# Threshold attention with a feed-forward block on one core: earlier front ends, one product with v a round later, and q and k turned in other rounds

## The chip, the cores and the metric

The kernel runs on one core of a Trainium2 chip. The metric is the device time of one execution in microseconds (us). Before the change three runs gave 907.24, 909.61 and 909.83 us, median 909.61. The profiled execution spans 909.1 us.

## The reference

Eight batches of eight heads, 576 positions, 64 numbers per head, all float32. Then a feed-forward block over the 4,608 tokens of 512 numbers.

```python
scores = (1 / sqrt(64)) * q @ k.T                     # per batch and head, 576 x 576
thresh = max(scores, axis=-1) - tau
scores = where(scores >= thresh, scores, -1e9)
attn   = exp(scores - max(scores))
attn   = attn / (sum(attn) + 1e-9)
x      = attn @ v                                     # -> tokens x 512
h      = x @ w_in                                     # 512 -> 1024
solu   = h * softmax(h)
ln     = (solu - mean(solu)) / sqrt(var(solu) + 1e-6) * g_ln
out    = ln @ w_out                                   # 1024 -> 512
```

The weights w_in, w_out and g_ln arrive as 64-bit numbers and are converted in the kernel.

## The kernel before

All five engines follow one order, written out by hand in a loop of rounds (`while True`, L748). A slot is 128 query rows of a pair of heads; there are 18 per batch (`PER`), 144 in all (`NS`). In each batch four pairs of heads have two slots for the first 256 rows (kind 0), two for the next 256 (kind 1), and two last slots (kind 2) hold the remaining 64 rows of all four pairs. The 64 last rows of every head, named `ends` in the code, are called front ends below, after the words that describe the change.

Round `rnd` does this, in program order. PE turns some blocks of q and k into the spare columns of the score banks (`turn`, L269) and computes the scores of slot `rnd` (`scores`, L396). DVE finds each row's negated threshold (`maxes`, L413), ACT makes the ramp (`ramp`, L424) and the exponentials with their sums (`exps`, L433). Between the ramps of the two heads the turned blocks are copied out (`keeps`): q by L302 and L306, k by L327, the front ends by L343 and L347. These copies are divided between ACT and DVE, and stay wholly on ACT up to round 16 (`eased`). POOL normalises the slot of the round before (L443), DVE transposes it in 32 x 32 blocks (L455), and after the second slot of a unit SP issues four transfers that put the blocks into the order of the product with v (`wT<-T`, L466, 288 KB each).

The score banks are single (`s0`, `s1`): the next round's turns and scores wait until the ramps of this round have read them. The two other pairs of banks (`p0`, `p1`) are handed out by `take` and given back by `pairs_free`.

A unit is the two slots of one pair. Its product with v (`attend`, L491) is due `LAG_PV` = 3 rounds after its second slot; for the first two units one round more (`pv_due`, L687). Products with v come on PE after the round's scores and its feed-forward quarter, and may share a round with a quarter of the first kind only. When the four units of a batch and kind are done, two feed-forward tiles of 128 tokens become ready. A tile has four quarters, one per round: two of h = x w_in (L545) and two of the product with w_out (L647). Between them lie an exponential (L567), statistics on DVE (L588), a chain of small operations on POOL, the normalisation on ACT (L609) and on DVE (L614), a swap of halves by transfers (`V<-u`, L625) and a transposition (L635). So most rounds have a quarter, and some have none.

When a batch's q and k are turned is fixed by `preps` (L693): each pair has an earliest round `at` and four pieces, k in 3 and 1 blocks, one of front ends and 4 of q. A round takes pieces in order while its seven spare blocks (`SPARE`) last. A round in which a tile is in its second half takes none as long as the pair's first slot is more than four rounds off.

At the start `load_qk(0, 0)` loads q on SP's queue and k on ACT's, in halves of two heads; after the first half come the front ends of all eight heads (L135), and after these the second halves. Then tau is loaded (L724), and the first three weight pieces on ACT's queue. `whole_pair(0)` turns all of pair 0 in one go, into a pair of banks of its own; its copies need the scale that DVE derives from tau (`scl`, L174). Pairs 1 to 3 of batch 0 are turned whole in rounds 0, 2 and 4. During rounds 0 to 15 DVE also converts one weight piece per round (L221 to L247), each loaded three rounds ahead.

Of the kernel before, what the change touches and what calls it, by code (L numbers as in the profile page):

```python
# [16 lines left out]
P = 128  # L17
# [3 lines left out]
def kernel(  # L21
# [27 lines left out]
    nc = tc.nc  # L49
    B, H, S, D = q.shape  # L50
    DM, DFF = w_in.shape
    SM = 512
    ST = S - SM
    NP = H // 2
# [5 lines left out]
    ROWS = (slice(0, 64), slice(64, P))  # L60
# [15 lines left out]
    tau_t = const.tile([P, 1], F32, name="tau_t")  # L76
# [14 lines left out]
    ends = {}  # L91
# [27 lines left out]
    def load_one(b, hf, nm, queue=None):  # L119
        d = halves.setdefault((b, hf), {})  # L120
        hs = slice(4 * hf, 4 * hf + 4)
        src, rows = {"q": (q, ROWS[0]), "k": (k, ROWS[1])}[nm]
        d[nm] = loads.tile([P, 4, 4, D], F32, tag=nm, name=nm)

        parts = [slice(0, 2), slice(2, 4)] if b == 0 and hf == 0 else [slice(0, 4)]
        for x, part in enumerate(parts):
            queue = nc.scalar if nm == "k" and x + 1 < len(parts) else nc.sync
            queue.dma_start(
                out=d[nm][:, part].rearrange("p h t d -> p h (t d)"),
                in_=src[b, hs, 0:SM, :][part].rearrange("h (p t) d -> p h (t d)", t=4),  # L130
            )
            if hf == 0 and x == 0:
                if b not in ends:
                    ends[b] = loads.tile([P, H, D], F32, tag="ends", name="ends")
                queue.dma_start(  # L135
                    out=ends[b][rows], in_=src[b, :, SM:S, :].rearrange("h p d -> p h d")
                )

    def load_qk(b, hf):
        load_one(b, hf, "q")  # L140
        load_one(b, hf, "k")
# [52 lines left out]
    def piece(x):  # L194
        if x < 2 * NP:
            c, hf = divmod(x, 2)
            cols = slice(512 * hf, 512 * hf + 512)
            return w_in[P * c : P * c + P, cols], w1[:, c, cols], W_UNIT
        c = x - 2 * NP
        return w_out[P * c : P * c + P], w2[:, 2 * c], gs[:, c : c + 1]  # L200
# [4 lines left out]
    def weight_load(x):  # L205
        raw = work.tile(
            [P, 512], I64 if wide else F32, tag=("xh2", "xh3", "uT")[x % 3], bufs=1, name="raw"
        )
        queue = nc.scalar if x < 3 else nc.sync
        queue.dma_start(out=raw, in_=piece(x)[0])  # L210
        raws[x] = dict(raw=raw)
# [79 lines left out]
    def q_item(i, ts=slice(0, 4)):  # L291
        src, h0 = source(i)
        qT = pair(i)["qT"].rearrange("p (t r k) -> p r t k", t=4, r=2)
        n = ts.stop - ts.start

        def make(spare, x):
            for t in range(n):
                turn(spare, x + t, lambda r, y: src["q"][ROWS[r], h0 + y, ts.start + t])

        def keep(spare, x, r):  # L300
            if r == 0 or spare.get("eased"):
                nc.scalar.activation(  # L302
                    out=qT[:, r, ts], in_=seen(spare, r, x, n), func=AF.Copy, scale=scl
                )
            else:
                nc.vector.tensor_scalar(  # L306
                    out=qT[:, 1, ts], in0=seen(spare, 1, x, n), scalar1=scl, scalar2=None,
                    op0=ALU.mult,
                )

        return n, make, keep
# [5 lines left out]
    def k_item(i, ts=slice(0, 4)):  # L317
        src, h0 = source(i)
        to = k_parts(i)
        n = ts.stop - ts.start  # L320

        def make(spare, x):
            for t in range(n):
                turn(spare, x + t, lambda r, y: src["k"][ROWS[r], h0 + y, ts.start + t])

        def keep(spare, x, r):
            (nc.vector.tensor_copy if r and not spare.get("eased") else nc.scalar.copy)(  # L327
                out=to[:, 4 * r + ts.start : 4 * r + ts.stop],
                in_=seen(spare, r, x, n).rearrange("p t (k c) -> p t c k", c=2),
            )  # L330

        return n, make, keep

    def e_item(i):
        src, h0 = source(i)
        last = k_parts(i)[:, NK - 1]

        def make(spare, x):
            turn(spare, x, lambda r, y: ends[i // NP][ROWS[r], 2 * (i % NP) + y])

        def keep(spare, x, r):
            if r == 0:
                nc.scalar.activation(  # L343
                    out=pair(i)["qe"], in_=seen(spare, 0, x, 1)[:, 0], func=AF.Copy, scale=scl
                )
            else:
                (nc.scalar.copy if spare.get("eased") else nc.vector.tensor_copy)(  # L347
                    out=last, in_=seen(spare, 1, x, 1)[:, 0].rearrange("p (k c) -> p c k", c=2)
                )

        return 1, make, keep
# [329 lines left out]
    PER = NS // B  # L681
    LAG_PV = 3

    pv_due = []
    for s, (b, kind, hp, r) in enumerate(slots):
        if r == 1:
            pv_due.append((s + LAG_PV + (s < 4), (b, kind, hp)))  # L687

    def first_slot(i):
        return PER * (i // NP) + 2 * (i % NP)  # L690
# [2 lines left out]
    preps = []  # L693
    for i in range(NP, NPAIR):
        b, hp = divmod(i, NP)
        at = 13 + 2 * hp if i < 2 * NP - 1 else PER * (b - 1) + (6 + 3 * hp if hp < 3 else PER - 1)
        preps += [
            (at, 3, lambda i=i: k_item(i, slice(0, 3)), i),
            (at, 1, lambda i=i: k_item(i, slice(3, 4)), i),
            (at, 1, lambda i=i: e_item(i), i),  # L700
            (at, 4, lambda i=i: q_item(i), i),
        ]

    load_at = {}
    for b in range(1, B):
        r = PER * (b - 1)

        for at, job, hf, what in (
            (-1 if b > 1 else 11, load_one, 0, "q"),
            (1 if b > 1 else 9, load_one, 0, "k"),  # L710
            (7 if b > 1 else 13, load_one, 1, "k"),
            (9 if b > 1 else 15, load_one, 1, "q"),
            (11 if b > 1 else 17, load_v, 0, (0,)),
            (13 if b > 1 else 19, load_v, 0, (1, 2)),
            (PER + 3, load_v, 1, (0,)),
            (PER + 5, load_v, 1, (1, 2)),
        ):
            load_at.setdefault(r + at, []).append(
                lambda b=b, job=job, hf=hf, what=what: job(b, hf, what)
            )  # L720

    with tc.manual_schedule():
        load_qk(0, 0)
        nc.scalar.dma_start(out=tau_t, in_=tau.partition_broadcast(P))  # L724
        weight_load(0)
        constants()
        for x in range(1, 3):
            weight_load(x)
        load_qk(0, 1)
        nc.sync.dma_start(out=g_rows, in_=g_ln.rearrange("(c p) -> c p", p=P))  # L730
        whole_pair(0)
# [16 lines left out]
        while True:  # L748
# [70 lines left out]
            elif step == ("h", 1):  # L819
# [8 lines left out]
                at = rnd + 4 if more or not ready else rnd + 6  # L828
# [16 lines left out]
            if attending is not None:  # L845
                attend(attending)
                attended(attending)
                b, kind, hp = attending
# [56 lines left out]
```

## Time and profile before

| stretch (us) | PE busy | DVE busy | ACT busy | granted PE clock | DMA share |
|---|---|---|---|---|---|
| 10 to 20 | 5.66 | 7.14 | 6.63 | 0.89 | 0.81 |
| 20 to 30 | 6.24 | 9.82 | 8.48 | 0.67 | 0.74 |
| 50 to 60 | 5.75 | 9.93 | 7.56 | 0.84 | 0.90 |
| 100 to 110 | 10.00 | 8.37 | 7.09 | 1.00 | 0.76 |
| 120 to 130 | 8.73 | 8.02 | 8.74 | 1.00 | 0.68 |
| 150 to 160 | 10.00 | 6.76 | 7.25 | 1.00 | 1.01 |
| 190 to 200 | 8.60 | 2.91 | 2.84 | 0.83 | 1.03 |

Each row is ten microseconds; a busy time near ten names the engine that is the bound there. The granted clock is the mean share of full speed at which PE ran. The DMA share is the mean busy share of the 16 transfer engines. Lines of a timeline read: start, length, engine, source line, operation, tile written and read, shape, count, and in brackets the idle time before it with what ended that. One matmul instruction of float32 leaves two records, so counts of records are twice those of instructions.

### The profile page before, as it was taken

Reading aid. Unit: us, or ns where it says so; the run is one execution under the profiler, and the core shown is the slowest. Engines: PE = TensorE matmul, PEld = TensorE weight load, DVE = VectorE, ACT = ScalarE, POOL = GpSimd, SP = SyncE. Lnnn points to the kernel's source line nnn. Section 1 sums busy time; section 2 is a strip of 40 time slices with the busy share of each in tenths; the row PEclk is TensorE's granted clock in tenths of the full one; section 3 lists DMA queues with packets and bytes.
Section 4 is the critical chain, followed back from the end, with each engine's and each line's share of the span. In section 5 each row is a group of like instructions: output and inputs, shape, how many; then the busy total and the mean of one; then the engine's idle time right before and its main releaser. Section 6 shows DMA issues by size and latency. Waiting matters only on the chain. (4 is left out here: it accounts for less than half of the span.)

```text
span 909.1 us, 39662 instructions
## 1 busy us (share of the span) xinstructions
PE 852.8 (94%) x17089; PEld 653.6 (72%) x17089; DVE 679.3 (75%) x1307; ACT 591.6 (65%) x1239; POOL 453.8 (50%) x870
## 2 busy tenths in 40 slices
PE   4667799989999999999999999999999999999997
PEld 3444567878668787877788776888878778777555
DVE  4999877868767877787767777777777777777351
ACT  4867776757666766677757776777767777666121
POOL 1645555545645555555545455555555555555120
PEclk8679899999999999999999999999999999999999
DMA  7999979776867777777767777776877756766322
GB/s 222 251 224 255 212 186 208 183 173 155 196 144 181 172 166 184 180 174 166 185 161 173 175 161 170 183 172 158 191 175 176 177 136 152 169 143 139 81 48 48
DMA packets 95470, 154.61 MB, mean 170 GB/s; under 512 B 27192, under 2 KB 69184, under 8 KB 95296
## 3 DMA queue, kind: packets, MB, share of 16 engines
q1 hardware_dynamic: 93920, 150.12, 70.7%
q8 instruction: 134, 2.20, 1.1%
q10 hardware_dynamic: 1376, 1.97, 0.7%
q14 instruction: 40, 0.33, 0.1%
HBM read 46.14 MB, written 9.44 MB: 61 GB/s over the span
## 5 line engine op out<-in xcount | busy, mean ns | idle before, releaser
L413 DVE CUSTOM_DVE_ANT_0 w<-s_ps,tau_t 128x576 f32<-128x576 f32 x288 | 206.7, 755 | 159.2 <-PE s_ps L396 125.8
L424 ACT ACTIVATE w<-s_ps,nth 128x576 f32<-128x576 f32 x288 | 207.7, 744 | 122.0 <-DVE nth L413 99.3
L647 PE MATMUL o_ps<-w,uT 64*64 64x256 f32 x4608 | 270.5, 376 | 2.9 <-issue 1.8
L647 PEld LDWEIGHTS o_ps<-w,uT 64*64 64x64 f32 x4608 | 231.4, 133 | 48.8 <-issue 11.4
L545 PE MATMUL h_ps<-w,xh 64*64 64x512 f32 x1856 | 222.3, 593 | 3.4 <-issue 3.4
L443 POOL TENSOR_SCALAR w<-w,sm 128x576 f32<-128x576 f32 x288 | 218.2, 770 | 14.3
L433 ACT ACTIVATE w<-w,ntau 128x576 f32<-128x576 f32 x288 | 220.2, 772 | 0.0
L455 DVE STREAM_TRANSPOSE T<-w 128x576 f32<-128x576 f32 x288 | 205.7, 750 | 4.4 <-POOL w L443 4.0
L491 PEld LDWEIGHTS pv<-wT,v 64*64 64x64 f32 x5760 | 174.3, 138 | 38.5 <-issue 23.5
L396 PE MATMUL s_ps<-kT,qT 64*64 64x64 f32 (+1 forms) x2048 | 175.8, 421 | 15.0 <-ACT w L424 13.1
L491 PE MATMUL pv<-wT,v 64*64 64x128 f32 (+1 forms) x5760 | 176.1, 267 | 10.2 <-DMA wT<-T 6.2
L545 PEld LDWEIGHTS h_ps<-w,xh 64*64 64x64 f32 x1856 | 120.8, 134 | 87.2 <-issue 56.2
L440 POOL TENSOR_SCALAR sm<-sm 128x2 f32<-128x2 f32 x144 | 36.2, 252 | 277.6 <-ACT w L433 274.9
L441 POOL TENSOR_TENSOR sm<-sm,mone 128x2 f32<-128x2 f32 x144 | 107.9, 749 | 12.0
L396 PEld LDWEIGHTS s_ps<-kT,qT 64*64 64x64 f32 x2048 | 67.8, 138 | 23.7 <-ACT w L424 19.4
L609 ACT ACTIVATE V<-u,nb,rs 128x1024 f32<-128x1024 f32 x36 | 44.7, 1241 | 52.6 <-POOL nb L599 52.6
L513 ACT COPY xh<-pv 128x256 f32<-128x256 f32 x64 | 23.8, 373 | 73.8 <-PE pv L491 73.8
L433 ACT ACTIVATION_READ_ACCUMULATOR w<-w,ntau 128x1 f32 x288 | 56.8, 197 | 0.0
L558 DVE TENSOR_REDUCE hm<-h_ps 128x1 f32<-128x1024 f32 x36 | 43.0, 1194 | 12.7 <-PE h_ps L545 6.8
L573 DVE TENSOR_TENSOR u<-h_ps,u 128x1024 f32<-128x1024 f32 x36 | 42.8, 1190 | 10.3 <-ACT u L567 10.3
L635 DVE STREAM_TRANSPOSE uT<-V 128x1024 f32<-128x1024 f32 x36 | 43.8, 1217 | 8.9 <-DMA V<-u 8.8
L567 ACT ACTIVATE u<-h_ps,hm 128x1024 f32<-128x1024 f32 x36 | 40.3, 1119 | 13.8 <-DVE hm L558 8.0
(74 smaller groups left out, 620.0 us busy)
## 6 DMA issues: line engine op xcount, KB each, us to landing
wT<-T SPq DMA_DIRECT2D x288, 288.0 KB, 5.7
V<-u SPq DMA_DIRECT2D x144, 64.0 KB, 3.6
out_dram<-ob SPq DMA_DIRECT2D x72, 128.0 KB, 3.1
v<-in_v_dram SPq DMA_DIRECT2D x16, 512.0 KB, 6.2
v<-in_v_dram SPq DMA_DIRECT2D x32, 256.0 KB, 6.0
q<-in_q_dram SPq DMA_DIRECT2D x15, 512.0 KB, 6.8
k<-in_k_dram SPq DMA_DIRECT2D x15, 512.0 KB, 6.4
raw<-in_moe_w_out_dram SPq DMA_DIRECT2D x8, 512.0 KB, 6.8
```

What stands on the lines that cost most here:

```text
L396: nc.tensor.matmul(out=ps[h][ROWS[y], ks], lhsT=lhsT, rhs=d["kT"][ROWS[h], ks], start=True, stop=True,)
L413: nc.vector.tensor_tensor_reduce(out=w, in0=ps[:, 0:S], in1=tau_t.to_broadcast([P, S]), scale=1.0, scalar=BIG, op0=ALU.add, op1=ALU.min, a ...
L424: nc.scalar.activation(out=d["w"][x], in_=d["ps"][x][:, 0:S], func=AF.Prelu, bias=d["nth"][x], scale=-1.0, alpha=1.0e30,)
L433: nc.scalar.activation(out=w, in_=w, func=AF.Exp, bias=ntau, scale=1.0, accum_out=sm[:, x : x + 1])
L441: nc.gpsimd.tensor_tensor(out=sm, in0=sm, in1=mone, op=ALU.pow)
L443: nc.gpsimd.tensor_scalar(out=w, in0=w, scalar1=sm[:, x : x + 1], scalar2=1.0, op0=ALU.mult, op1=ALU.mult)
L455: nc.vector.transpose(out=T[:, :, r, h, :], in_=w)
L491: nc.tensor.matmul(out=to, lhsT=d["v"][ROWS[u], h0 + h, m ^ 4 * u if m < 8 else m], rhs=rhs, start=m == 0, stop=m == NK - 1,)
L545: mm = nc.tensor.matmul(out=h[ROWS[y], f], lhsT=x[ROWS[r], c, ROWS[y]], rhs=w1_parts[ROWS[r], c, part ^ r], start=part == 0 and c == 0, st ...
L609: nc.scalar.activation(out=V, in_=u, func=AF.Identity, bias=nb, scale=rs)
L635: nc.vector.transpose(out=uT, in_=d["V"].rearrange("p y (m x) -> p m y x", x=32))
L647: nc.tensor.matmul(out=d["o"][ROWS[z], 512 * r : 512 * r + 256], lhsT=d["uT"][ROWS[r], m].rearrange("p y x -> p (y x)"), rhs=w2[ROWS[r], m ...
```

## The change

Three things are moved; nothing is computed differently.

First, the start. Tau's load goes ahead of q and k on ACT's queue. The front ends are loaded in two parts for batch 0: those of heads 0 and 1 where all eight were, the other six on SP's queue after the first weight loads and before `load_qk(0, 1)`. It is meant to bring what the first pair needs sooner.

Second, `(s < 4)` becomes `(s < 6)`: the third unit's product with v is due four rounds after its second slot and not three, in round 9 and not 8, which gives its transfers more time.

Third, new earliest rounds for the turns of batches 1 and 2; from batch 3 on they are as before. By the written order, in batch 1 pair 2 moves from rounds 18 and 19 to 20 and 21, and pair 3 from 19 and 20 to 21 and 22. In batch 2 pair 1 moves from rounds 28 and 29 to 30 and 31, pair 2 from 30 and 31 to 34 and 35, pair 3 from 35 and 38 to 39 and 40. It is meant to keep turns out of rounds that have no feed-forward quarter.

```diff
-                queue.dma_start(
-                    out=ends[b][rows], in_=src[b, :, SM:S, :].rearrange("h p d -> p h d")
-                )
+                load_ends(b, nm, slice(0, 2) if len(parts) > 1 else slice(0, H), queue)
+
+    def load_ends(b, nm, of, queue):
+        src, rows = {"q": (q, ROWS[0]), "k": (k, ROWS[1])}[nm]
+        queue.dma_start(
+            out=ends[b][rows, of], in_=src[b, of, SM:S, :].rearrange("h p d -> p h d")
+        )
...
-            pv_due.append((s + LAG_PV + (s < 4), (b, kind, hp)))
+            pv_due.append((s + LAG_PV + (s < 6), (b, kind, hp)))
...
-        at = 13 + 2 * hp if i < 2 * NP - 1 else PER * (b - 1) + (6 + 3 * hp if hp < 3 else PER - 1)
+        if b == 1:
+            at = (13, 15, 20, 20)[hp]
+        else:
+            at = PER * (b - 1) + ((6, 12, 16, 21) if b == 2 else (6, 9, 12, 17))[hp]
...
     with tc.manual_schedule():
+        nc.scalar.dma_start(out=tau_t, in_=tau.partition_broadcast(P))
         load_qk(0, 0)
-        nc.scalar.dma_start(out=tau_t, in_=tau.partition_broadcast(P))
         weight_load(0)
         constants()
         for x in range(1, 3):
             weight_load(x)
+        for nm in ("q", "k"):
+            load_ends(0, nm, slice(2, H), nc.sync)
         load_qk(0, 1)
```

## Prediction

> **What bounds the kernel now.** I read the page first, busy time and the 40 slices, then busy time by stretch, then the engines' timelines over the first 260 us.
>
> ```profile
> PE 852.8 (94%) x17089; PEld 653.6 (72%) x17089; DVE 679.3 (75%) x1307; ACT 591.6 (65%) x1239; POOL 453.8 (50%) x870
> ...
> PE   4667799989999999999999999999999999999997
> ...
> DVE  4999877868767877787767777777777777777351
> ```
> ```profile
> 0.00:110.00 110.00, 73.16 (x1263) 48.46 (x1267) 93.69 (x194) 73.44 (x162) 53.37 (x83) 0.81 0.91 231
> ```
> ```profile
> 110.00:250.00 140.00, 132.06 (x2846) 103.87 (x2842) 103.97 (x205) 95.33 (x205) 73.22 (x140) 0.99 0.80 186
> ```
> ```profile
> 250.00:800.00 550.00, 544.34 (x11373) 431.62 (x11369) 424.10 (x824) 382.36 (x800) 292.64 (x573) 1.00 0.74 170
> ```
> The columns of a stretch are its length, then busy time of PE, weight loads, DVE, ACT and POOL, granted clock, DMA share and GB/s. So there are three stages. To about 105 us DVE is the bound (93.69 of 110 us, and most of the rest is the start): each round holds 5.35 us of DVE work, of which nearly half is the conversion of a weight piece. From 110 to 250 us PE is busy all but 7.9 us. From 250 us on PE is full (5.7 us of 550 idle, gaps put down to "issue"). A microsecond taken from the DVE path before 105 us moves all that follows; one taken from PE work after it counts too; idle PE time before 105 us is worth nothing by itself.
>
> Where does DVE wait in the first stage? At the start, and at two places for the scores:
>
> ```profile
> 7.45 0.15 DVE L174 TENSOR_SCALAR scl<-tau_t 128x1 f32<-128x1 f32 x1 [7.45 <-DMA tau_t<-in_tau_dram]
> ...
> 45.45 0.76 DVE L413 CUSTOM_DVE_ANT_0 w<-s_ps,tau_t 128x576 f32<-128x576 f32 x1 [0.67 <-PE s_ps L396]
> 63.24 0.76 DVE L413 CUSTOM_DVE_ANT_0 w<-s_ps,tau_t 128x576 f32<-128x576 f32 x1 [1.81 <-PE s_ps L396]
> ```
> PE's timeline says what held the scores in each case:
>
> ```profile
> 5.13 1.10 PE L269 MATMUL tp<-ident,k 64*64 64x64 f32 x32
> 8.33 0.49 PE L269 MATMUL tp<-ident,ends 64*64 64x64 f32 x8 [2.09 <-DMA ends<-in_q_dram]
> 10.00 2.20 PE L396 MATMUL s_ps<-kT,qT 64*64 64x64 f32 x16 [1.19 <-DVE kT L347]
> ...
> 56.97 0.43 PE L491 MATMUL pv<-wT,v 64*64 64x128 f32 x4 [2.72 <-DMA wT<-T]
> 58.58 3.74 PE L491 MATMUL pv<-wT,v 64*64 64x128 f32 x66 [1.18 <-DMA wT<-T]
> ```
> The first two heads' q and k are turned by 6.2 us, then PE stands until the front ends of q have landed at 8.3. At 57 us the product of unit (0,0,2) with v heads PE's queue and waits 3.9 us for its transposed weights; the next scores are queued behind it, and DVE loses 1.81 us.
>
> **What the skill says.** "DMA: Bandwidth & Descriptors", under "Why small descriptors are slow (HBM only)", says that pieces of 256 B carry a fixed overhead, 27% of the bus time. A front end is 512 rows of 256 B, and the trace agrees in kind: q's 128 KB were issued at 1.23 us and needed until 8.3, while 256 KB of k issued at 0.72 had landed 4.0 us later. The same page, "Issuing engines are not separate DMA queues": transfers of SP and ACT interleave on the same engines, so an earlier place only helps what is small or early. "TensorE: Matmul & The Clock Gate", "HAM oscillation": PE idle for some 3.4 us falls to a slower clock. Here the products with v took 3.74 us at 191.83 after an idle 1.53, and 2.23 at 163.19 with none, so a shorter gap than the page's is enough here.
>
> **Part 1, start.** Tau goes first on ACT's queue; only two heads of each front end (32 KB instead of 128) go ahead of the second half of q and k; six heads follow. Gain: the front ends can no longer be the last to land, since q lands at 4.1 and k at 4.7 (issue plus 3.4 and 4.0), k perhaps 0.3 later behind tau's issue (0.63 us). k's turns end at about 6.2 instead of the front ends starting at 8.33, so up to 8.33 - 6.2 = 2.1 us. Tau, landed at 7.4 before, must not take its place: first in its queue and 0.5 KB, it should be there by 4. I take 2.0 us, bounds 1.0 and 2.3. It is on the path, because scores, the first maxima (DVE, 12.23) and all rounds of the DVE-bound stage follow in a chain. Costs: two more issues on SP (0.7 us each), off the path while q and k of the second half land only at 10.0 and 10.6. In the built program transfers share eight completion lanes in turn, so the six heads wait for tau and for q, which are early, and k of the second four heads now waits for a lane that is free only when q of heads 2 and 3 has landed, about 10 us instead of 5.2. It is used at 23 us, and landed at 17.6 before: hidden. The six heads are needed by the turns of pair 1, before at 13.65, now at 11.6; the scores behind those turns wait for a ramp until 15.5 - 2 = 13.5, so a landing up to 13 is hidden. What could give part of it back is DMA, whose share is about 1.0 between 30 and 50 us; but transposed weights issued at 29.6 landed 6.6 us later at 36.2, 3.3 us before their use at 39.5, and these issues move along with the rounds.
>
> **Part 2, third unit's product from round 8 to round 9.** It then follows the scores of round 9, whose ramp ends at 58.3 (both before the shift of part 1). Those scores end at 59.5 instead of 63.3, so DVE's 1.81 us go. The product starts near 59.5, when the last quarter of its weights has landed (issue about 51.3 plus 7.3 is 58.6), so its own wait goes too. Give-back: one round later the next unit's product comes directly behind in PE's order, in round 10. Before, it started at 67.35 with 1.7 us to spare for the scores behind it (they ended at 72.1, DVE came to them at 73.9); its weights, issued until 62.9, land no earlier through this part. So of the 1.81 up to 0.5 may return as a wait. I take 1.5, bounds 0.8 and 1.9. The output copy on ACT moves with it, and the first feed-forward tile needs only the fourth unit: no cost.
>
> **Part 3, the turns.** No work is added or removed. Pairs 2 and 3 of batch 1 leave rounds 18 to 20 for 20 to 22; of batch 2, pair 1 leaves rounds 28 and 29 for 30 and 31, pair 2 goes from 30 and 31 to 34 and 35, pair 3 from 35 and 38 to 39 and 40. Rounds 19, 28, 29 and 38 have no feed-forward quarter, so PE comes to their end early and waits for ramps, which stand behind the copies of the turned blocks on ACT:
>
> ```profile
> 127.54 0.33 PE L269 MATMUL s_ps<-ident,k 64*64 64x64 f32 x4 [0.89 <-ACT kT L327]
> ...
> 178.80 0.33 PE L269 MATMUL s_ps<-ident,q 64*64 64x64 f32 x4 [0.93 <-ACT qe L343]
> ...
> 191.00 0.44 PE L491 MATMUL pv<-wT,v 64*64 64x128 f32 x4 [1.53 <-DMA wT<-T]
> 191.83 3.74 PE L491 MATMUL pv<-wT,v 64*64 64x128 f32 x66 [0.40 <-DMA wT<-T]
> ```
> Rounds 18 to 20: turns of 0.58 and 0.82 us leave PE, copies of 0.79 leave ACT. But round 19's ramps also stand behind the normalisation on ACT, which waits for POOL until 124.56 and moves with DVE by only 0.7 to 0.9. I get the ramp's end at 126.65 for 128.1: 1.5 us sooner. Rounds 21 and 22, where PE has no idle time, take 0.82 + 0.72 = 1.54 us more. Net 0.
>
> Rounds 28 to 30: the scores of round 30 come 2.1 us sooner. Then a wait takes the place: the product of round 30 needs weights whose transfer is issued behind DVE's transposition (178.96) and the swap of the normalised tile (179.06), which move by 0.8 only. PE would wait about 2.8 us instead of 1.53, and 0.8 us is left, against 0.58 + 0.47 added to rounds 34 to 40 (0.58 of pair 2 and the net 0.47 of pair 3, the rest being exchanged) with 0.4 recovered in round 38. Net +0.2, bounds -1.0 and +1.5. The sum for part 3 is taken as 0.
>
> **Sum.** 909.6 - 2.0 - 1.5 + 0 = 906.1 us.
>
> **Rivals.** (a) The turns pay: PE's idle time in rounds 19, 20, 28, 29 and 38 (0.89 + 0.31 + 0.93 + 0.30 + 0.17 + 0.40 + 0.87 = 3.9 us) largely goes, without the new wait. With 2.5 of it: 903.6. Against it speaks the wait at 191. (b) The start's gain is lost to DMA, or unit 4's wait returns all of part 2: 909.6 - 1.0 - 0.8 + 0.5 = 908.3, within 0.3%. For it: the DMA share. Against: weight loads issued at 67 landed in 3.6 us, so no backlog builds up before then. (c) Slower: the moved turns (2.9 us of PE work in all) land in full rounds, PE stands still longer at 191 and runs cold for a further stretch (1.5 us, as 3.74 against 2.23), 0.5 of part 2 returns, and only 1.8 is gained before: 909.6 + 2.9 + 1.5 + 0.5 - 1.8 = 912.7.
>
> **Chances.** Forecast 0.57, (a) 0.12, (b) 0.21, (c) 0.10. Runs of the kernel before lie within 907.2 to 909.8, so any of these blurs by about 1 us. Faster by over 0.3% means under 906.9: most of the forecast and (a), 0.66. Slower means over 912.3: 0.10. The rest, 0.24, is no change. The range takes in (a) and (b) and stops short of (c): 903.4 to 910.0.
>
> **What would show it.** Right: front-end turns at about 6.2 us with no long wait; first maximum near 10.2; no wait of DVE for scores in round 9; DVE's 110 us of work done some 3.5 us sooner; idle PE at about 127 and 179 smaller, at about 190 larger; rounds 250 us on unchanged in length. Wrong: tau or k as the new last lander, a wait of the fourth unit of over 1 us in which DVE stands still, or a gap at the third batch's pair in 30 to 40 that grows.

## The result and the profile after

The changed kernel took 902.5 us (median of four runs, 901.9 to 904.4) against 909.7 for the kernel before on the same chip (907.2 to 910.2): ratio 0.993, interval 0.9906 to 0.9953. That is 7.2 us by the medians, where 3.5 were forecast, and 0.9 us below the low end of the range. Three later measurements of the same kernel gave 0.9969, 1.0005 and 0.9942. So there are two questions: what the change does, and why one measurement does not tell it.

First the pair of traces on record. The page after, busy time and then the 40 slices of PE and DVE:

```profile
PE 847.8 (94%) x17089; PEld 658.4 (73%) x17089; DVE 680.1 (76%) x1307; ACT 591.9 (66%) x1239; POOL 452.7 (50%) x870
...
PE   5667889999899999999999999999999999999997
...
DVE  5999878878677777777777877777877877787351
```
Busy time by stretch after, with the columns of the prediction (length, PE, weight loads, DVE, ACT, POOL, granted clock, DMA share, GB/s):

```profile
0.00:110.00 110.00, 76.03 (x1349) 51.73 (x1353) 95.64 (x195) 75.44 (x166) 53.48 (x84) 0.80 0.91 238
110.00:250.00 140.00, 131.49 (x2883) 105.93 (x2879) 107.08 (x210) 97.91 (x209) 74.87 (x143) 1.00 0.81 191
250.00:800.00 550.00, 545.58 (x11433) 438.76 (x11429) 426.96 (x829) 383.12 (x801) 294.84 (x579) 1.00 0.73 170
```
More DVE work fits into the first 110 us (95.64 for 93.69) and the next 140 (107.08 for 103.97). From 250 us on PE is as full as before. So the time came for the most part from the first 250 us, as the argument wanted. Where in them, the timeline of PE after tells, at the places shown of before:

```profile
4.91 1.13 PE L273 MATMUL tp<-ident,q 64*64 64x64 f32 x32 [4.91 <-DMA q<-in_q_dram]
5.79 1.10 PE L273 MATMUL tp<-ident,k 64*64 64x64 f32 x32
6.64 0.46 PE L273 MATMUL tp<-ident,ends 64*64 64x64 f32 x8
...
64.94 0.43 PE L495 MATMUL pv<-wT,v 64*64 64x128 f32 x4 [1.66 <-DMA wT<-T]
66.23 2.07 PE L495 MATMUL pv<-wT,v 64*64 64x128 f32 x66 [0.86 <-DMA wT<-T]
...
122.78 0.33 PE L273 MATMUL s_ps<-ident,k 64*64 64x64 f32 x4 [0.94 <-ACT w L428]
...
133.08 0.27 PE L273 MATMUL s_ps<-ident,k 64*64 64x64 f32 x1 [1.50 <-issue]
133.19 1.19 PE L400 MATMUL s_ps<-kT,qT 64*64 64x64 f32 x13
134.11 3.70 PE L549 MATMUL h_ps<-w,xh 64*64 64x512 f32 x32
...
173.91 0.33 PE L400 MATMUL s_ps<-kT,qT 64*64 64x64 f32 x4 [0.94 <-ACT w L428]
...
183.99 0.44 PE L495 MATMUL pv<-wT,v 64*64 64x128 f32 x4 [0.77 <-DMA wT<-T]
185.48 2.07 PE L495 MATMUL pv<-wT,v 64*64 64x128 f32 x66 [1.06 <-DMA wT<-T]
```
The front ends follow k at 6.64 without a wait. The long wait at 57 us is gone; the fourth unit's product, at 64.94, waits 1.66 + 0.86 us, but DVE does not stand for it. The waits for ramps at 122.78 and 173.91 are as long as their counterparts before (0.89 and 0.93): the rounds became shorter, the waits stayed. The product of round 30, at 183.99, still waits 1.83 us, but then runs in 2.07, not 3.74. And there is a gap of 1.50 us at 133.08 that ends on nothing but "issue".

A good clock for such a pair is the first maximum of each round on DVE (L413, after L417). The difference of its start, after less before, changes by -1.72 us at the start, -1.90 at round 9, +1.07 at round 16, -2.39 in rounds 18 and 19 (given back: 0.84 in 22 and 23), -3.67 in rounds 28 to 31, +1.13 in rounds 34 to 40, +0.77 at round 41 and -2.02 at round 42. From there to the end it moves between -7.3 and -9.1 and ends at -8.5. Each of these looks like a finding. The experiments show which are (the 1.07 at round 16 is none: from the first maximum of round 15 to that of 16 seven traces with the third product in round 8 take 7.28 us on average, thirteen with it in round 9 7.31): most sums that follow are means of such distances between first maxima over twenty traces, one for each kernel and measurement.

### The profile page after: what moved, and what is told of

It is laid out like the page before. It is cut to its first block, busy times and chain, and to the rows that moved or that the text cites. A ratio compares the mean times of both kernels' runs of the same rounds, so it can differ in the third digit from the quotient of the medians.

```text
span 900.4 us, 39661 instructions
## 1 busy us (share of the span) xinstructions
PE 847.8 (94%) x17089; PEld 658.4 (73%) x17089; DVE 680.1 (76%) x1307; ACT 591.9 (66%) x1239; POOL 452.7 (50%) x870
## 5 line engine op out<-in xcount | busy, mean ns | idle before, releaser
L417 DVE CUSTOM_DVE_ANT_0 w<-s_ps,tau_t 128x576 f32<-128x576 f32 x288 | 206.6, 755 | 151.3 <-PE s_ps L400 122.9
L651 PEld LDWEIGHTS o_ps<-w,uT 64*64 64x64 f32 x4608 | 227.9, 133 | 51.2 <-ACT xh L517 9.6
L549 PEld LDWEIGHTS h_ps<-w,xh 64*64 64x64 f32 x1856 | 127.0, 134 | 80.8 <-issue 34.0
L495 PE MATMUL pv<-wT,v 64*64 64x128 f32 (+1 forms) x5760 | 173.9, 264 | 7.2 <-DMA wT<-T 5.1
L400 PEld LDWEIGHTS s_ps<-kT,qT 64*64 64x64 f32 x2048 | 70.2, 139 | 23.7 <-ACT w L428 21.0
```

The source lines that it names most:

```text
L400: nc.tensor.matmul(out=ps[h][ROWS[y], ks], lhsT=lhsT, rhs=d["kT"][ROWS[h], ks], start=True, stop=True,)
L417: nc.vector.tensor_tensor_reduce(out=w, in0=ps[:, 0:S], in1=tau_t.to_broadcast([P, S]), scale=1.0, scalar=BIG, op0=ALU.add, op1=ALU.min, a ...
L495: nc.tensor.matmul(out=to, lhsT=d["v"][ROWS[u], h0 + h, m ^ 4 * u if m < 8 else m], rhs=rhs, start=m == 0, stop=m == NK - 1,)
L549: mm = nc.tensor.matmul(out=h[ROWS[y], f], lhsT=x[ROWS[r], c, ROWS[y]], rhs=w1_parts[ROWS[r], c, part ^ r], start=part == 0 and c == 0, st ...
L651: nc.tensor.matmul(out=d["o"][ROWS[z], 512 * r : 512 * r + 256], lhsT=d["uT"][ROWS[r], m].rearrange("p y x -> p (y x)"), rhs=w2[ROWS[r], m ...
```

## The experiments

Every measurement stands beside runs of the kernel before on the same chip; "runs" counts those of the kernel itself, and the ratio is to the kernel before.

| what | runs | median us | ratio (interval) |
|---|---|---|---|
| whole change, on record | 4 | 902.5 | 0.9930 (0.9906 to 0.9953) |
| whole change, second | 14 | 906.0 | 0.9969 (0.9948 to 0.9990) |
| whole change, third | 22 | 907.7 | 1.0005 (0.9987 to 1.0024) |
| whole change, fourth | 13 | 904.8 | 0.9942 (0.9920 to 0.9964) |
| start alone | 22 | 905.2 | 0.9970 (0.9951 to 0.9989) |
| split front ends alone | 22 | 908.5 | 1.0008 (0.9986 to 1.0030) |
| third unit's product alone | 22 | 905.7 | 0.9964 (0.9942 to 0.9985) |
| turns of batch 1 alone | 22 | 908.8 | 0.9997 (0.9974 to 1.0019) |
| turns of batch 2 alone | 22 | 906.3 | 0.9975 (0.9956 to 0.9993) |
| all turns alone | 14 | 908.1 | 0.9993 (0.9971 to 1.0015) |
| start and product, beside the third | 12 | 902.7 | 0.9952 (0.9920 to 0.9983) |
| start and product, beside the fourth | 15 | 903.3 | 0.9938 (0.9908 to 0.9968) |
| change without batch 1's turns, beside the third | 22 | 905.8 | 0.9984 (0.9965 to 1.0003) |
| change, batch 1 from 19 and 21, beside the fourth | 22 | 905.2 | 0.9950 (0.9933 to 0.9967) |
| change, batch 1 from 20 and 22, beside the fourth | 18 | 903.3 | 0.9931 (0.9911 to 0.9951) |
| product of round 30 later, alone | 22 | 903.9 | 0.9950 (0.9930 to 0.9971) |
| the same with the whole change | 15 | 902.0 | 0.9920 (0.9897 to 0.9943) |
| start, both products later | 7 | 900.7 | 0.9901 (0.9865 to 0.9937) |
| the last one with batch 1 from 20 and 22 | 7 | 900.7 | 0.9925 (0.9888 to 0.9963) |

The ratio with its 95% interval is the one on record; it is not the quotient of the two medians, and the two differ by up to about 0.001, in one row (the last but one) by 0.0036.

### The same kernel again

No edit; three more measurements on three chips.

> The changed kernel once more, in the same rounds as the three kernels beside it. Theory A (the three parts add up, as measured each alone: medians -3.0 for the start, -3.2 for the product one round later, -0.9 and -2.3 for the turns of the two batches): 909.4 less about 7 to 9, so 900 to 902.5, a ratio of 0.990 to 0.993. Rival B (the first measurement of -7.2 is part chance, as single runs of these kernels lie up to 10 us apart; what the traces support is 1.0 for the start, 2 to 3 for the product, 0.5 to 1 for the turns): a ratio of 0.994 to 0.996, 4 to 5.5 us faster.

> The changed kernel a third time, beside three kernels that have only part of the change. Theory A (the true gain is about that of the prediction; the first -7.2 of four runs was a lucky sample, the second gave -3.0): 2.5 to 4.5 us faster, ratio 0.995 to 0.997. Rival B (the first measurement stands): 6 to 8 us faster, ratio 0.991 to 0.993.

> The changed kernel on one more chip. Theory A (rounds 20 to 23 hold a loss of about 3 us in most executions, which the first measurement happened to miss): 0 to 4 us faster than before, and rounds 20 to 23 take 21.5 to 22 us in its trace. Rival B (the first measurement is what the kernel does): 6 to 8 us faster, rounds 20 to 23 about 18.9 us.

Measured: 0.9969, 1.0005 and 0.9942. With the first, the mean of the four ratios is 0.9962, 3.5 us of 909. But the first and the third do not agree within their intervals, so the same change is worth something else from one measurement to the next, by more than its runs scatter within one. Single runs of the kernel before ranged from 900.0 to 917.4 us in all; its medians lay between 906.4 and 909.9. The second fell short of both its theories, though its interval takes in part of rival B's 0.994 to 0.996. Neither theory held of the third, which gave nothing, nor of the fourth (5.3 us by the ratio, between the two).

### The start

Alone, as in the diff of the change; then with tau's load back behind q and k:

```diff
     with tc.manual_schedule():
-        nc.scalar.dma_start(out=tau_t, in_=tau.partition_broadcast(P))
         load_qk(0, 0)
+        nc.scalar.dma_start(out=tau_t, in_=tau.partition_broadcast(P))
         weight_load(0)
```


> Part 1 alone. Theory A (the parts add, each worth what the trace pair shows round by round): the first maximum at 10.5 us for 12.2, this 1.7 us kept through the DVE-bound rounds, total 1.2 to 2.0 us faster than before. Rival B (the parts add to the predicted 3.5 and the other 3.7 us are gaps of the kind 'issue' that fell out well in the new runs, whatever the part): every one of the kernels with one part, this one too, shows a gain of its own plus the same kind of scatter, so about 2 us here as well, and no part is worth more than its predicted size.

> Of the start, the split front ends alone; tau's load stays behind q and k on its queue. Theory A (the front ends were what came last in three of the old traces, and tau's load, ahead of q and k, makes q land 0.7 to 0.9 us later, 4.91 for 4.2): first maximum at 10.0 to 10.6, as with both or sooner, 2.5 to 3.5 us faster than before, as the whole start alone was (-3.0). Rival B (tau then is what lands last, at 7 us or later, as it did in some traces of the kernel before): turns of the front ends at about 6.2, yet the first maximum at 11 to 11.5, 1 us faster than before or less.

The whole start alone measured 0.997, 2.7 us and so above theory A's 1.2 to 2.0, which its interval takes in; the split front ends alone 1.0008. The timeline of all engines in the kernel with the split alone (PE, then DVE's scale and first maximum):

```profile
5.85 0.47 PE L273 MATMUL tp<-ident,ends 64*64 64x64 f32 x8
...
8.85 0.15 DVE L178 TENSOR_SCALAR scl<-tau_t 128x1 f32<-128x1 f32 x1 [8.85 <-DMA tau_t<-in_tau_dram]
...
12.68 0.76 DVE L417 CUSTOM_DVE_ANT_0 w<-s_ps,tau_t 128x576 f32<-128x576 f32 x1 [2.37 <-PE s_ps L400]
```
The front ends are turned at 5.85, sooner than in the changed kernel, and it is no use: tau lands at 8.85 and takes their place. Rival B is right. With the old start tau was not early elsewhere either. The timeline of the kernel that has only batch 1's turns moved:

```profile
6.17 0.49 PE L269 MATMUL tp<-ident,ends 64*64 64x64 f32 x8
...
7.62 0.15 DVE L174 TENSOR_SCALAR scl<-tau_t 128x1 f32<-128x1 f32 x1 [7.62 <-DMA tau_t<-in_tau_dram]
```
Here the front ends landed at 6.17 of themselves, and tau decided. And the changed kernel's answer to it:

```profile
4.14 0.15 DVE L178 TENSOR_SCALAR scl<-tau_t 128x1 f32<-128x1 f32 x1 [4.14 <-DMA tau_t<-in_tau_dram]
```
Six traces with the old start have their first maximum between 10.55 and 12.23 us, mean 11.26; thirteen with the new one between 10.41 and 10.85, mean 10.66. The trace of before was the latest of the six. So the start brings 0.6 us on average and takes the scatter away. The split alone brings none of it. Tau alone was not tried; in the two of the six traces where the front ends landed at 8.1 and 8.3 it could not have helped. The timed runs of the start alone show more, 1.0 to 4.4 us by the interval; the traces do not explain the rest.

### The third unit's product one round later

```diff
-            pv_due.append((s + LAG_PV + (s < 4), (b, kind, hp)))
+            pv_due.append((s + LAG_PV + (s < 6), (b, kind, hp)))
```


> Part 2 alone. Theory A: the first maximum of round 9 comes 1.9 us sooner; the scores of round 16 give about 1.1 of it back if that loss belongs to this part (the quarter of round 15 on a slower clock), so 0.8 to 1.9 us faster. Rival B: 1.5 us. If the loss at round 16 is seen here it belongs to part 2; if not, to the earlier start or to chance.

Measured 0.9964, 1.4 to 5.3 us faster, which takes in rival B's 1.5 and a part of theory A's 0.8 to 1.9. Left in round 8, the product makes DVE lose anything from nothing to 4.7 us over seven traces, 2.4 on average. One with a larger loss than the 1.81 of before is the kernel in which only the product of round 30 is moved; PE's timeline, then DVE's:

```profile
56.00 0.58 PE L491 MATMUL pv<-wT,v 64*64 64x128 f32 x4 [3.82 <-DMA wT<-T]
57.62 3.89 PE L491 MATMUL pv<-wT,v 64*64 64x128 f32 x66 [1.05 <-DMA wT<-T]
```
```profile
63.22 0.76 DVE L413 CUSTOM_DVE_ANT_0 w<-s_ps,tau_t 128x576 f32<-128x576 f32 x1 [3.87 <-PE s_ps L396]
```
In round 9 that is over, but a wait can come back two rounds later, in round 11, behind the fourth unit's product. DVE's timeline of the changed kernel with the product of round 30 later as well:

```profile
71.75 0.76 DVE L417 CUSTOM_DVE_ANT_0 w<-s_ps,tau_t 128x576 f32<-128x576 f32 x1 [1.80 <-PE s_ps L400]
```
From the first maximum of round 8 to that of round 12 it takes 23.98 us on average in seven traces with the product in round 8 and 22.15 in thirteen with it in round 9 (8 to 9: 7.76 and 5.37; 9 to 12: 16.22 and 16.78). So 2.39 us are won and 0.56 returned: 1.8 us.

### The turned pairs

```diff
         if b == 1:
-            at = (13, 15, 20, 20)[hp]
+            at = (13, 15, 17, 17)[hp]
         else:
             at = PER * (b - 1) + ((6, 12, 16, 21) if b == 2 else (6, 9, 12, 17))[hp]
```
These are the changed kernel's rounds and, in the line added, the old ones for batch 1; the old ones for batch 2 are `(6, 9, 12, 17)`. First each batch moved alone, then both, with nothing else of the change.

> Part 3 for batch 1 alone. Theory A: rounds 18 to 20 lose 2.4 us and rounds 21 to 25 give back 0.6, so 1.5 to 2.0 us faster: a turned block costs less in a full round (0.5 and 0.3 us seen for the two rounds) than its first start to last end in the trace (0.82 and 0.72), because that includes the overlapped latency of the last matmul. Prediction as on record, rival B: 0 plus or minus 0.5.

> Part 3 for batch 2 alone. Theory A: rounds 28 and 29 lose 1.5 us; the transferred weights of the product in round 30 land 2 us sooner and PE, which waits no longer than before, stays warm, so that product takes 2.1 for 3.7 us; rounds 34 to 40 give back 1.1: 2 to 3 us faster. Rival C (the landing moved because of the batch 1 change or the earlier start, and the clock by chance[...]): the product of round 30 stays at 3.7 us, and the kernel is within 1 us of before. Prediction as on record, rival B: 0.2 slower.

> The kernel before with the moved turns of both batches, start and products as before. Theory A (the turns pay as measured each alone, -0.9 and -2.3): 3 to 3.5 us faster, ratio 0.996 to 0.997. Rival B (the prediction's sum: nothing): within 1 us of before. Rival C (the turns of batch 2 pay 0.7 to 1 us, those of batch 1 nothing, because what rounds 18 and 19 save goes into full rounds 21 and 22): 0.5 to 1.5 us faster. In the trace all expect the first maxima of rounds 18 and 19 to come 1.1 to 1.3 us sooner each and rounds 22 and 23 to take 0.5 and 0.3 us more.

Measured 0.9997, 0.9975 and 0.9993. Batch 1 alone did nothing (rival B). Batch 2 alone gave theory A's 2.3 us, but in its trace, taken of its slowest run (912.86 us), not for its reason: the product of round 30 still took 3.74 us. PE's timeline there:

```profile
191.75 3.74 PE L491 MATMUL pv<-wT,v 64*64 64x128 f32 x66 [0.77 <-DMA wT<-T]
```
Both together can't be told from nothing. Then the other way round, the change without the turns, beside the whole change:

> The new start and the product of the third unit one round later, all turned pairs in their old rounds. Theory A (the moved turns cost: ten traces give rounds 17 to 27 a mean of 57.9 us with the turns of batch 1 moved and 56.7 without, rounds 27 to 41 a mean of 80.7 with those of batch 2 moved and 80.1 without): 1 to 2 us faster than the changed kernel of the same rounds, about 5 us faster than before. Rival B (start and product each measured about 3 us alone and add up): 6 us faster than before. Rival C (the turns are worth what they measured alone, -1.2): about 1 us slower than the changed kernel.

> New start and product of the third unit one round later, no turned pair moved, on the same chip as the changed kernel. Theory A (the moved turns cost): 2 to 4 us faster than the changed kernel of the same rounds, 4 to 6 faster than before; rounds 20 to 23 take 17.2 to 18.2 us. Rival B (the turns are worth about 1 us): 1 us slower than the changed kernel.

> The changed kernel with the turned pairs of batch 1 in their old rounds. Theory A (moving them puts 142 short products and 54 turns in one row ahead of a place where PE stands for instructions: that gap measured 1.5 to 3.2 us in five traces with them moved, 0.8 to 1.8 in five without, and scores and a feed-forward quarter ran slow behind it, which takes back the 1.9 us that rounds 17 to 20 save): the same as the changed kernel or up to 1.5 us faster, and a gap of 0.8 to 1.8 us in round 20 or 21. Rival B (the gaps are chance): 1 to 1.5 us slower than the changed kernel, since the 1.9 us of rounds 17 to 20 are lost and 0.8 regained.

Without any turn moved the kernel was 4.8 us faster than the whole change in the third measurement (0.9952 against 1.0005) and as fast in the fourth (0.9938 against 0.9942). Without batch 1's turns it was 1.9 us faster than the whole change, but the intervals overlap. The 2 to 4 us over the whole change that theory A named for the fourth measurement did not show. So the turns did no good beside start and product, and in the third measurement they did harm.

The traces tell where. Rounds 17 to 20 take 16.09 us in ten traces with batch 1's turns in their old rounds and 14.16 in seven with them moved: 1.93 us saved, steadily. Rounds 20 to 23 take 17.65 and 21.03: 3.38 us lost, and not steadily, from 18.9 to 22.0. The timeline of PE in the second measurement of the whole change shows the loss:

```profile
133.68 0.37 PE L273 MATMUL s_ps<-ident,k 64*64 64x64 f32 x1 [2.62 <-issue]
133.69 0.38 PE L400 MATMUL s_ps<-kT,qT 64*64 64x64 f32 x3
133.84 0.31 PE L273 MATMUL s_ps<-ident,k 64*64 64x64 f32 x1
133.85 2.22 PE L400 MATMUL s_ps<-kT,qT 64*64 64x64 f32 x13
135.66 4.12 PE L549 MATMUL h_ps<-w,xh 64*64 64x512 f32 x32
```
The turns themselves are short. But PE stands 2.62 us near the end of their row, waiting for nothing that the timeline shows, and what follows runs on a slow clock (granted 0.77 over the next 6 us): scores 2.22 for 1.19, the quarter 4.12 for 3.70. It is the same place as the gap of 1.50 in the trace on record, behind which nothing ran slow. Counted in matmul records from the start, 17 of the twenty traces have a gap of 0.4 us or more here, after 1,870 or 1,871 of them; the other three have theirs 128 or 256 records earlier. Before, and in the kernel with start and product alone, it falls into the product with v; PE's timeline of the latter beside the third measurement:

```profile
134.22 0.97 PE L495 MATMUL pv<-wT,v 64*64 64x64 f32 x50 [0.87 <-issue]
```
With batch 1's turns moved the gap measured 1.50, 1.85, 2.08, 2.08, 2.27, 2.62 and 3.17 us in seven traces; with the old rounds the longest gap here measured 0.83 to 1.79 us in ten. What precedes it is then a row of nothing but short instructions: 72 products of 64 columns and 28 turns. Before it was a part of the 72 only.

What PE waits for can be read from the records of transfers, which the timeline does not show. The page of the changed kernel lists a queue of instructions:

```profile
## 3 DMA queue, kind: packets, MB, share of 16 engines
...
q8 instruction: 134, 2.20, 1.1%
```
Each packet is 16,384 bytes, and 134 of them stand against 17,089 matmuls and as many weight loads: one for about 128 of each. In the twenty traces there are 102 gaps of 0.4 us or more on PE after 100 us that end on "issue". Every one ends 1.24 to 1.70 us after such a packet has landed, where less than 9% of all moments lie so. So what PE waits for there is its next instructions. In the seven traces with batch 1's turns moved, the packet ahead of the gap started 1.51 us before PE ran out (gap of 1.50) to 0.36 us after (gap of 3.17), and PE went on 2.6 to 3.0 us after that start. A row of short instructions uses up a packet fast: 128 of these products take about 2.2 us, by an estimate from 142 in 2.39 us. Why a packet starts when it does is not shown.

Two kernels break that row in different ways:

```diff
-            at = (13, 15, 20, 20)[hp]
+            at = (13, 15, 19, 21)[hp]
```
```diff
-            at = (13, 15, 20, 20)[hp]
+            at = (13, 15, 20, 22)[hp]
```


> The changed kernel with the last two pairs of batch 1 turned from rounds 19 and 21 on, not both from 20 on: behind the 72 products of round 20 stand 20 turns in place of 28, and those of round 19 stand ahead of it. Theory A (the long row of short instructions ahead of the place where PE stands for instructions makes the gap long, and what follows runs on a slow clock): a shorter gap, 1 to 2 us, rounds 20 to 23 at 18.5 to 20 us, about 2 us faster than the changed kernel less the part of the 1.9 us of rounds 17 to 20 that goes back. Rival B (any move of these turns behind round 19 brings the long gap): rounds 20 to 23 at 21.5 us or more, as fast as the changed kernel.

> The changed kernel with the last pair of batch 1 turned from round 22 on and the one ahead of it from 20 on: behind the 72 products of round 20 stand 16 turns (0.3 us) in place of 28, and the rest after the next feed-forward quarter. Theory A (the length of the row of short instructions sets the gap): a gap between those without moved turns (0.8 to 1.8) and those with (2.1 to 3.2), so 1.5 to 2.2 us, rounds 20 to 23 at 19 to 21 us, 1 to 2 us faster than the changed kernel. Rival B (the gap is long wherever turns follow these products): 21.5 us or more in rounds 20 to 23, no difference from the changed kernel.

Measured 0.9950 and 0.9931, against 0.9942 for the whole change beside them. With rounds 20 and 22 the place of the gap comes to lie in a feed-forward quarter, whose instructions are long; PE's timeline:

```profile
131.40 1.12 PE L549 MATMUL h_ps<-w,xh 64*64 64x512 f32 x6
133.00 3.21 PE L549 MATMUL h_ps<-w,xh 64*64 64x512 f32 x25 [0.48 <-issue]
```
0.48 us are left of it, less than either theory said; rounds 20 to 23 take 18.33 us and rounds 17 to 20 keep their 14.10, so in that trace the move pays 1.3 us against the old rounds (16.09 + 17.65 less 14.10 + 18.33). With 19 and 21 the gap stayed at 1.88, the clock held, and rounds 20 to 23 took 18.54, but half of the 1.9 us went back (15.08). In the timed runs neither differs from the whole change by more than the intervals, since that chip's trace of the whole change had a short gap too (1.85, rounds 20 to 23 at 19.2 us). That a row of short instructions makes the gap long agrees with all traces here, but rests on one trace of each of these two kernels where the row was broken.

Batch 2's turns repeat this on a smaller scale. Rounds 27 to 32 are 1.25 us shorter with them moved (28.06, nine traces, against 29.31, seven), and rounds 32 to 41 are 1.8 us longer (52.16 against 50.35). Of the latter, 1.16 come up to round 40, with the moved turns; most of the rest, 0.65 at round 41, fits the next gap, after record 4,030, which the pair moved to rounds 39 and 40 now precedes: 1.3 us on average in ten traces, 0.9 in ten with the old rounds.

### The wait in round 30

```diff
-            pv_due.append((s + LAG_PV + (s < 6), (b, kind, hp)))
+            pv_due.append((s + LAG_PV + (s < 6 or s == 27), (b, kind, hp)))
```
This moves the product that waits near 190 us to round 31, in the kernel before (with `s < 4`) and in the changed one.

> The kernel before, with only the product with v of unit (1,1,0) in round 31 instead of 30. Theory A (the wait of 1.53 + 0.40 us in round 30 goes, and the product runs at 2.1 to 2.2 us, not 3.74): 2 to 3.5 us faster than before. Rival B (a wait for a ramp takes its place, since rounds 28 and 29 keep their turns and their scores are late): 0.5 us faster or less, with an idle PE of more than 1 us in round 30 or 31.

> The changed kernel, and the product with v of unit (1,1,0), which stands in round 30 and waits there 1.1 to 1.9 us for its transposed weights, one round later, in round 31. Theory A (that wait is on the path, and the product sometimes runs cold behind it, 3.7 us for 2.1): 1.5 to 3 us faster than the changed kernel of the same rounds, since PE has no idle time behind it to make up for it. Rival B (the wait moves to the next instruction, the scores of round 31, which wait for a ramp instead): 0 to 0.5 us faster, with a new wait of 1 us or more in round 30 or 31 in the trace.

Measured 0.9950 alone, and with the change 0.9920, against 0.9969 for the change beside it: both times some 4.5 us. PE's timeline of the first:

```profile
184.36 0.62 PE L269 MATMUL s_ps<-ident,k 64*64 64x64 f32 x26 [0.40 <-ACT w L424]
...
190.74 3.70 PE L545 MATMUL h_ps<-w,xh 64*64 64x512 f32 x32
194.17 2.23 PE L491 MATMUL pv<-wT,v 64*64 64x128 f32 x71
```
The wait of 1.9 us is gone, no other takes its place, and the product runs at full speed. Theory A held, and the gain was larger than its upper end; from round 27 to 41 the traces show 2.2 us of it (77.48 in three traces, 79.67 in seven, batch 2's turns in their old rounds). So one condition in one line, at a wait that the prediction had quoted, does as much as the whole change.

### All that pays

> New start, product of the third unit and that of unit (1,1,0) each one round later, no turned pair moved. Theory A (the moved turns bring nothing here, since the wait in round 30 that they were to shorten is gone): 1 to 2.5 us faster than the changed kernel with that same product late (which was 7.1 us faster than before), so 8 to 9.5 us faster than before. Rival B (the turns still help rounds 18 to 20 and 28, 29): 5 to 6.5 us faster than before.

> New start, product of the third unit and that of unit (1,1,0) each one round later, batch 1's last two pairs turned from rounds 20 and 22 on, batch 2's pairs in their old rounds. Theory A (sum of means of the traces: start 0.7, third product 2.0, late product 3.3, the turns 1.9 in rounds 17 to 20 less about 0.9 in rounds 20 to 23): 7 us faster than before, ratio 0.991 to 0.993, rounds 20 to 23 at 18 to 19 us. Rival B (the timed runs gave more for start and product than the traces, 3 us each alone): 9 to 10 us faster, ratio 0.989 to 0.990. Rival C (the gap in round 20 grows again): 21 us or more in rounds 20 to 23, 5 us faster at most.

Start and both products, no turn moved: 0.9901. With batch 1 from rounds 20 and 22 on as well: 0.9925. Their intervals overlap widely, and the comparison is across chips. By the ratio the times are those of theory A for both, 9.0 and 6.8 us, though the last kernel's rounds 20 to 23 took 19.4 us, not 18 to 19. The medians of the first differ by 5.7 us only (900.7 against 906.4), which would be its rival B; its seven runs do not decide. By the ratios either is faster than the whole change was on the average of four measurements (0.9962), the second within its interval.

## Why the prediction was right and wrong

**The bound.** Right: what was taken off DVE's path before 105 us moved what follows, and from 250 us on little happened but gaps that come and go. The largest is this one in the trace of before (one other trace has a gap there, of 0.79):

```profile
254.55 2.60 PE L647 MATMUL o_ps<-w,uT 64*64 64x256 f32 x43 [1.62 <-issue]
```
It makes most of the -2.02 at round 42, which is no work of the change: from the first maximum of round 41 to that of 42, 18 of the 19 other traces took 4.33 us, before 6.35.

**Start, -2.0.** Direction and mechanism right (turns of front ends behind k, first maximum at 10.51 for the 10.2 named), tau was the lander to be feared, and the split alone proved it. The size was wrong. It was read off one execution, in which the front ends landed at 8.3; in four of the six with the old start their turns began at 6.2 to 6.8, and tau came last or with them (6.7 to 7.6). The mean is 0.6. Also q came 0.66 us later with tau ahead (4.91 for 4.25), where only k had been given a delay, of 0.3. And the small pieces do not account for the late front ends: k's, as large and in the same pieces, landed 4.1 us after their issue in that very trace, about as fast as 256 KB of k (4.0). (One more reading was off: the transposed weights put at 29.6 and 36.2 us were issued at 28.8 and landed at 35.3; their slack was larger, and nothing hangs on it.)

**Third product, -1.5.** Right, and for its reason: 2.39 won, 0.56 returned in rounds 9 to 12 (the sum had allowed up to 0.5), 1.8 net, in the bounds. The 1.81 us of that one trace were less than the average loss of 2.4.

**Turns, 0.** This is the step that failed for the measurement on record. In its trace the turns brought 1.55 in rounds 18 to 23, and up to 3.67 less 1.13 = 2.5 in batch 2, where the sum said nothing and the bounds for batch 2 -1.0 to +1.5. (Its +0.2 for batch 2 is a gain by its own terms, 0.8 less 0.65; the run with batch 2's turns was told it as a loss.) Over all traces they brought nothing: batch 1's cost 1.3 us, batch 2's 0.5. Two terms were mis-sized. The 1.54 us that the turns were to cost rounds 21 and 22 are 0.84 by the distances of the first maxima plus whatever the gap at record 1,871 and the slow clock behind it add: next to nothing in the trace on record (1.50 us for 1.32), some 3 in others, and the prediction had put such gaps down as "issue" and left them alone. (The Trainium skill, "Runtime: NRT & Kernel Launch", in "Instruction fetch mechanics", says that engines refill their instruction memory in blocks of 16 KiB, 256 instructions, and that crossing into the next is mostly hidden. The packets of 16,384 bytes agree with the block; the gaps behind them, of 0.4 to 3.2 us, are not hidden.) And the wait in round 30 was to grow to 2.8 us; it did not (1.83 for 1.93 in the pair; 1.8 on average in nine traces with batch 2's turns moved, 1.9 in seven without), since the scores of round 30 came only 1.07 us sooner, not 2.1, and the weights about as much. What looked like a gain of 2.6 us at round 31 is mostly the clock behind that wait: 2.07 us for the product in nine of sixteen traces, 2.83 to 3.74 in seven, with waits of the same size and with either place of the turns. The Trainium skill, "TensorE: Matmul & The Clock Gate", in "What's actually happening", calls the warm-up at a kernel's start run-variable, since the clock's activity window runs free; these products behave as if that held in mid-kernel too.

**The spread.** "Any of these blurs by about 1 us" was the other wrong step. It rested on three runs of before that happened to lie close. Over four measurements the change gave 6.4, 2.8 and 5.3 us by the ratio, and once nothing. The two best are the two whose trace has a short gap in round 21 (rounds 20 to 23 at 18.9 and 19.2 us), the two others have 22.0 and 21.9. That makes the gap a likely cause of some 3 us of the difference; one trace for each measurement does not prove it, and why it should keep to a chip or a measurement is open.

**Rivals.** (a), the turns pay, gave nearly the time on record (903.6 for 902.5), but by another way than told: the waits for ramps that were to go are still there (0.94 at 122.78 and at 173.91). (b), 908.3 or a ratio of 0.9986, is nearest to the third measurement (1.0005), but the gain of the start was not lost to DMA; in the traces it was small from the outset. The forecast, 906.1 or a ratio of 0.9962, was met by the second measurement (0.9969) and by the mean of the four. That is in part luck: the traces give its three parts as a gain of 0.6, a gain of 1.8 and a loss of 1.8.

**What stays open.** The terms read from the traces do not make up that mean. Start and product together show 2.8 us (first maximum of round 17: 113.66 us in the five traces with the old start and the product in round 8, 110.87 in twelve with both new), and batch 1's turns lose 1.3 (rounds 17 to 27: 56.41 and 57.70), batch 2's 0.5 (rounds 27 to 41: 79.67 and 80.21). That leaves about 1 us of gain, where the timed runs show 3.5; where the other 2.5 us come from stays open. One trace stands for some twenty runs that differ by up to 10 us, so each of these means is uncertain by about half a microsecond or more; what else the runs hold was not found.

Three things of what "would show it" answered: front ends at once behind k, no wait of DVE in round 9, and DVE's work done sooner. Two answered no: the waits at 127 and 179 not smaller, the one at 190 not larger.

## What to carry to other kernels

Size a gain from a wait only after you know how that wait varies; what one trace promised was three times the mean in one place here (the start) and less than the mean in another (the third product). Look for the wait that has slack to be moved behind other work (the product of round 30), before you move work to shorten it. And do not add short instructions to a row of short ones on a full engine without a look at its "issue" gaps and at the packets of its instruction queue: here such gaps are fixed in the order of instructions, and one grew with the short row ahead of it.

## What was not expected of the hardware

PE runs out of instructions at fixed places of its order. In all twenty traces it stands after 4,030, 8,350 and 12,669 matmul records, to within one record and so some 4,320 apart, and in 17 of them after 1,870 or 1,871, for 0.4 to 3.2 us; where a second gap stands near one of these, it is 126 to 128 records off. The one at 8,350 measured 1.8 to 2.3 us in all twenty, and no edit here went near it. Each ends 1.24 to 1.70 us after a packet of 16,384 bytes of instructions has landed. A gap of up to 1.88 us at record 1,871 left the clock at full speed; four of the five from 2.08 us on were followed by a granted clock of 0.72 to 0.77 over the next 6 us, with slow scores and a slow quarter (4.1 to 5.2 us for 3.7), 1.4 to 1.9 us more. The longest, of 3.17, was not.
